# Zero products in TensorE's gaps, queries made token by token, and x in a ring of ten tiles, in a planned attention and GeGLU kernel

## The chip, the cores and the metric

One core of a Trainium2 chip runs the whole kernel. The metric is device time in microseconds of one execution; the time given for a kernel is the median of its runs. TensorE (PE) multiplies, VectorE (DVE), ScalarE (ACT) and GpSimd (POOL) work on elements, SyncE (SP) issues most DMAs.

## What is computed

A transformer block on x of 2048 tokens by 640, in bf16, with 32 query heads of 20 channels that share one key and one value head:

```python
q = (x @ wq).reshape(B, S, H, Dh).transpose(0, 2, 1, 3)     # H = 32, Dh = 20
k, v = x @ wk, x @ wv                                       # one head
p = softmax(einsum("bhqd,bkd->bhqk", q, k) * Dh ** -0.5)
A(x) = einsum("bhqk,bkd->bhqd", p, v).transpose(...) @ wo
B(x) = (gelu(x @ w_gate) * (x @ w_up)) @ w_down             # 640 -> 1536 -> 640
h = x + A(layernorm(x));  out = h + B(layernorm(h))
```

## The kernel before

**A program planned ahead.** The Python code holds a small model of the core. `_Plan` keeps a clock for each engine. A loop (the end of the kernel function) picks the engine that is free first and asks its `*_decide` function for the next piece of work; `commit` books it with an assumed cost, an assumed delay until others see the result, and its dependences. What comes out is a fixed order of instructions for each engine. `resolve` and `emit` turn the dependences into semaphore waits. The assumed costs only shape the order; on the chip each engine runs its list in that order and waits where a semaphore is not there yet. SP's list is in order as well. `PRM` holds the numbers that steer the choice (how many units may be open, how early work may start, ring sizes).

**The work.** The 16 tiles of 128 tokens are normalized (LN1: `ln_group`, `ln_stats`), written to `xn_tmp` and brought into channel-major form in `xn1T` by a DMA transpose. `kv_job` makes keys (`kT4`, four copies at partitions 0, 32, 64, 96) and values (`v_ext`, with a column of ones that yields the softmax's sum, and in three weights). The square root in LN1 is a power on POOL; while any power is outstanding (`pow_left`), `dve_ok` keeps DVE from exponentials, since the power and the 64-bit add are both POOL operations.

**Attention.** It is cut into 64 *units* of 256 query columns for each of four heads, each of 8 *packs* of two key tiles: 512 packs. A pack (`issue_qk`, L912) is eight products of 20 rows by 256 columns, in the four row groups of the array, into four PSUM banks. Each bank is a *tile* of 512 exponentials. Either ACT takes it (`act_tile`, L1266, into the ring `pa` of `NA` = 26 slots), or DVE does (`dve_tile`, L1325, one multiply and add into a 16-bit integer that is read as bf16, into the ring `pd` of `ND` = 9 slots), and POOL then adds two constants to it (L1405) so that three weighted versions cancel the error. The products with values (`issue_pv`, L975) are two per ACT tile and six per DVE tile, of 32 output columns each, so four run side by side in the column groups. A unit's sums lie in one bank, go to `osb`, are transposed by DMA to `onu`, divided (L634), collected in `onq`, transposed to `onT` and multiplied by `wo`.

**Side work.** Pieces of other products (`mm`, L502) fill PE between packs: queries, output projection, and per *batch* of tiles gate, up and down. `mm` splits each product of 128 weight columns in four of 32, one for each column group, which is also how the value products use the array. `SW` is the time the plan books for a change between the two ways. `q_job` makes the queries of a pair of units with the channels on the partitions: weights `wq`, moving operand `xn1T`, 20 of 32 columns used, so that the result can be copied straight into `qT`, of `NQ` = 3 slots. All 16 tiles of x stay in `xh`, to which first `wo`'s result (L676) and then the down product (L798) are added in place. LN2 puts its result in a buffer of its own, `xn2T`.

**The head and the tail.** x and the attention weights are loaded on the queues of SP and ACT at the start, the other weights on SP when the plan's clock for SP has passed 30 us. The tail is what is left once no pack is left: the last batches (tiles 12 and 13; 14; 15). Their gate and up products move 256 and 128 columns.

Of the kernel before, what the change touches and what calls it, by code (L numbers as in the profile page):

```python
# [37 lines left out]
class _Plan:  # L38
# [104 lines left out]
    def emit(self, name, eng, sems):  # L143
        done = 0
        for op, waits in zip(self.ops[name], self.waits[name]):
            for d in waits:
                if d.dma:
                    eng.wait_ge(d.sem, 16)
# [28 lines left out]
class _Job:  # L177
# [14 lines left out]
PRM = {  # L192
    "chunks": [[0], [1], [2, 3], [4, 5], [6, 7], [8, 9], [10, 11], [12, 13], [14], [15]],
# [3 lines left out]
    "NA": 26, "ND": 9, "NON": 4,  # L197
    "open": 3, "open_head": 3, "acc_head": 2, "w_head": 4, "w_max": 2, "w_tol": 600.0,
    "early": 530.0, "slack": 60.0, "open_r": 14, "press_a": 5, "press_d": 2, "v_min": 2,
    "q_ahead": 2, "lay": 0, "flex_d": 400.0, "pair_min": 4, "age": 3000.0, "pool_max": 3000.0,  # L200
    "stag_n": 3, "stag_w": 250.0,
    "quota": 3,
    "rate": 350.0, "w_tol0": 0.0, "w_max0": 2, "lag": 20, "quota0": 4, "quota_n": 16,
# [3 lines left out]
def bass_sequential_preLN__grouped_kv_mqa__glu_gated_geglu__prompt_kernel(  # L207
# [35 lines left out]
    NQ = 3  # L243
# [12 lines left out]
    xh = sb("xh", [P, NT, D], BF16)  # L256
    xn1T = sb("xn1T", [P, NC_D, S], BF16)
    xn2T = sb("xn2T", [P, NC_D, 1024], BF16)
    wq_sb = sb("wq_sb", [P, NC_D * D + 16], BF16)
# [6 lines left out]
    qT = sb("qT", [P, NQ, 512], BF16)  # L266
# [10 lines left out]
    ident = sb("ident", [P, P], BF16)  # L277
# [8 lines left out]
    ln_r = sb("ln_r", [P, 2, NT], F32)  # L286
    nwt = sb("nwt", [P, 4, NT], F32)
    pd16 = pd[:].bitcast(BF16)
# [33 lines left out]
    load("sp", xh[:, 0, :], x_view[:, 0, :], [("x", 0)], lat=2000)  # L322
    load("act", xh[:, 1, :], x_view[:, 1, :], [("x", 1)], lat=2200)
    load("sp", wk_v, cview(A_wk), ["wk"], lat=2500)
    load("act", wv_sb[:], cview(A_wv), ["wv"], lat=2500)
    load("sp", xh[:, 2:4, :], x_view[:, 2:4, :], [("x", 2), ("x", 3)], lat=2800)
    load("act", wq_v[:, :, 0:HALF], cview(A_wq)[:, :, 0:HALF], [("wq", 0)], lat=4000)
    load("sp", xh[:, 4:6, :], x_view[:, 4:6, :], [("x", t) for t in range(4, 6)], lat=4000)
    load("act", wq_v[:, :, HALF:D], cview(A_wq)[:, :, HALF:D], [("wq", 1)], lat=4500)
    load("sp", xh[:, 6:8, :], x_view[:, 6:8, :], [("x", t) for t in range(6, 8)], lat=5000)  # L330
    load("sp", xh[:, 8:12, :], x_view[:, 8:12, :], [("x", t) for t in range(8, 12)], lat=6000)
    load("sp", xh[:, 12:16, :], x_view[:, 12:16, :], [("x", t) for t in range(12, 16)], lat=8000)
# [4 lines left out]
    pool(lambda e: e.memset(warm[:], 0.0), 80, writes=["warm"])  # L337
    pool(lambda e: e.memset(halfc[:], 0.5), 80, writes=["halfc"])
    pool(lambda e: e.memset(wk_sb[:, NC_D * Dh:NC_D * Dh + 16], 0.0), 80, writes=["wkz"])
    pool(lambda e: e.memset(wq_sb[:, NC_D * D:NC_D * D + 16], 0.0), 80, writes=["wqz"])  # L340
# [3 lines left out]
    pool(lambda e: e.memset(ident[:], 0.0), 120, writes=["ident0"])  # L344
    pool(lambda e: e.affine_select(out=ident[:], in_=ident[:], compare_op=ALU.not_equal, fill=1.0, base=0,
                                   pattern=[[-1, P]], channel_multiplier=1), 320, ["ident0"], ["ident"])
# [10 lines left out]
    slots = {"xt": list(range(NXT)), "q": list(range(NQ)), "onT": list(range(4)), "osb": list(range(NOS)),  # L357
             "onu": list(range(NOS))}
# [21 lines left out]

    def ln_stats(ln, t, prio, then):
        key = ("x", t) if ln == 0 else ("h", t)

        def b(op):
            dve(lambda e: e.bn_stats(stats[:, ln, t, 6:12], xh[:, t, HALF:D]), 360, [key], [("st", ln, t, 1)],  # L385
                prio, c)
# [5 lines left out]
        dve(lambda e: e.bn_stats(stats[:, ln, t, 0:6], xh[:, t, 0:HALF]), 360, [key], [("st", ln, t, 0)], prio, b)  # L392

    def ln_group(ln, tiles, prio, done):
# [4 lines left out]
        if ln == 0:  # L399
            state["pow_left"] += 1  # L400

        def after_stats(op):
            cnt[0] += 1
            if cnt[0] == n:
                dve(lambda e: e.tensor_copy(ln_vb[:, ln, sl], mv[:, ln, sl, 1]), 65,
                    [("mv", ln, t) for t in tiles], [("vb", kk)], prio, c2)

        def c2(op):
            dve(lambda e: e.tensor_scalar_add(ln_veb[:, ln, sl], ln_vb[:, ln, sl], EPS), 65,
                [("vb", kk)], [("veb", kk)], prio, c3 if ln == 0 else n0)  # L410

        def c3(op):
            def pdone(op):
                state["pow_left"] -= 1
                c4(op)
            task(("pool",), lambda e: e.tensor_tensor(ln_denb[:, ln, sl], ln_veb[:, ln, sl], halfc[:, 0:n], ALU.pow),
                 700, L_POOL, [("veb", kk), "halfc"], [("den", kk)], prio, pdone)
# [4 lines left out]
        def n0(op):  # L422
            dve(lambda e: e.tensor_copy(va, ln_veb[:, ln, sl]), 65, [("veb", kk)], [("nv", kk)], prio, n1)

        def n1(op):
            dve(lambda e: e.tensor_scalar(ya.bitcast(I32), va.bitcast(I32), -0.5, 1597463007.0, ALU.mult, ALU.add),
                65, [("nv", kk)], [("ny", kk)], prio, newton(0))

        def newton(i):
            def s1(op):  # L430
                dve(lambda e: e.scalar_tensor_tensor(ta, va, -0.5, ya, ALU.mult, ALU.mult), 65,
                    [("nv", kk), ("ny", kk)], [("nt", kk)], prio, s2)

            def s2(op):
                dve(lambda e: e.tensor_tensor(ta, ta, ya, ALU.mult), 65, [("nt", kk), ("ny", kk)], [("nt", kk)],
                    prio, s3)

            def s3(op):
                dve(lambda e: e.scalar_tensor_tensor(ya, ta, 1.5, ya, ALU.add, ALU.mult), 65,
                    [("nt", kk), ("ny", kk)], [("ny", kk)], prio, newton(i + 1) if i < 2 else nden)  # L440
            return s1

        def nden(op):
            dve(lambda e: e.tensor_tensor(ln_denb[:, ln, sl], va, ya, ALU.mult), 65, [("nv", kk), ("ny", kk)],
                [("den", kk)], prio, c4)

        def c4(op):
            dve(lambda e: e.reciprocal(ln_r[:, ln, sl], ln_denb[:, ln, sl]), 75, [("den", kk)], [("lr", kk)],
                prio, c5)

        def c5(op):
            for t in tiles:
                norm(t)

        def norm(t):
            slot = []

            def then(op):
                s = slot[0]

# [4 lines left out]
                if ln == 0:  # L465
                    o = xn1T[:, :, t * P:(t + 1) * P]
                    wkeys = [("xn1T", t)]
                else:
                    o = xn2T[:, :, xcol[t]:xcol[t] + P]
                    wkeys = [("xn2T", xcol[t])]  # L470
# [4 lines left out]
            tk = _Task(("dve",), None, 350, L_DVE, [key, ("lr", kk)], [], prio, then, lambda: bool(slots["xt"]))  # L475

            def bind():
                s = slots["xt"].pop(0)
                slot.append(s)
                tk.fn = lambda e: e.tensor_scalar(xn_tmp[:, s, :], xh[:, t, :], mv[:, ln, t, 0:1],  # L480
                                                  ln_r[:, ln, t:t + 1], ALU.subtract, ALU.mult)
# [8 lines left out]
    xcol = {}  # L490
    for b, tl in enumerate(BATCHES):
        for i, t in enumerate(tl):
            xcol[t] = (b % 2) * 512 + i * P

# [3 lines left out]
    def mm(o, l, r, st, sp):  # L498
        def fn(e, b):
# [3 lines left out]
            return ins  # L503
        return fn

    def col4(a):
        return lambda q: a[:, 32 * q:32 * q + 32]

    def kv_job(tiles):
# [3 lines left out]
        for c in range(NC_D):  # L513
            pieces.append((mm(lambda b: bank(b, n), (lambda c: lambda q: wk_sb[:, c * Dh:c * Dh + 32])(c), xn1T[:, c, t0 * P:t0 * P + n],
                              c == 0, c == NC_D - 1), c_mm(n), [("xn1T", t) for t in tiles] + ["wk", "wkz"]))
# [30 lines left out]
    for ci, tl in enumerate(CHUNKS):  # L546
        nt = len(tl)
        G = 2 // nt
        for k in range(NG // G):
            units.append({"id": len(units), "chunk": ci, "tiles": tl, "groups": list(range(k * G, (k + 1) * G)),  # L550
                          "left": list(range(NT // 2)), "q": None, "qop": None, "acc": None, "npk": 0,
# [3 lines left out]
    def q_job(ua, ub):  # L555
        tl, gs = ua["tiles"], ua["groups"] + ub["groups"]
        n = len(tl) * P
        t0 = tl[0]
        pieces = []
        for gi, g in enumerate(gs):  # L560
            for c in range(NC_D):
                pieces.append((mm((lambda gi: lambda b: ps[:, b * 512 + gi * n:b * 512 + (gi + 1) * n])(gi),
# [964 lines left out]
```

## Time and profile before

| | |
|---|---|
| median of 3 runs | 824.82 us (818.34 to 826.53) |
| the profiled execution | 823.09 us, its span 821.2 us |
| mean granted TensorE clock | 0.954 |
| PE, DVE, ACT, POOL busy | 737.2, 678.4, 699.3, 567.9 us |
| products on PE | 18392, each with a weight load |
| packs (eight products each), tiles of ACT and DVE | 512; 1287 and 761 |

The profile is of one execution. A *span* runs from the first to the last instruction; what the execution takes beyond it lies around the instructions. *Idle before* is the time an engine stood still ahead of an instruction, and the *releaser* is what ended that; "issue" means that the profile shows nothing it waited for. The *chain* follows the work that ended last back from the end. *PEclk* is the TensorE clock that was granted, as a share of full speed. A product's record is longer than the time until the next may start, so the busy time of PE overstates how full the array is.

### The profile page before, as it was taken

To read this page: it belongs to the slowest core of one execution; us is meant where nothing else is said; L and a number is where in the kernel's file an instruction comes from. 1 tells how busy PE (TensorE), PEld (TensorE's weight loads), DVE (VectorE), ACT (ScalarE), POOL (GpSimd) and SP (SyncE) were. 2 spreads that over 40 slices of the span, in tenths; PEclk is the share of its full clock that TensorE was granted. 3 is DMA by queue.
4 is the path that set the end of the run, shared out by engine and by line. 5 is a ranking of instruction groups with operands and counts; after the bars stand their busy time and mean duration, and the time that the engine had idled before them with its cause. 6 is when DMAs were issued, how large, how long until landed. Compare 5 with 4: busy or idle time off the path is not lost.

```text
span 821.2 us, 41718 instructions
## 1 busy us (share of the span) xinstructions
PE 737.2 (90%) x18392; PEld 408.6 (50%) x18392; DVE 678.4 (83%) x1389; ACT 699.3 (85%) x1231; POOL 567.9 (69%) x1424
## 2 busy tenths in 40 slices
PE   2788999988898999999999998999998999999976
PEld 2444444444443455355555444455545554465874
DVE  5756789998888888898899989998899899899532
ACT  1888799988888999999998999999999899999411
POOL 2265788887877786688887785788887784678100
PEclk9776899998988999999999999999999999999999
DMA  8880000001100201100101000100101010111110
GB/s 207 106 320 9 17 10 18 9 9 25 21 13 10 25 10 20 25 10 10 34 10 50 10 10 19 26 9 10 34 10 42 18 26 4 26 18 38 31 29 20
DMA packets 60452, 27.57 MB, mean 34 GB/s; under 512 B 51440, under 2 KB 58992, under 8 KB 60272
## 3 DMA queue, kind: packets, MB, share of 16 engines
q1 hardware_dynamic: 58160, 23.89, 13.6%
q8 instruction: 146, 2.39, 1.2%
q10 hardware_dynamic: 2112, 1.01, 0.5%
q14 instruction: 34, 0.28, 0.1%
HBM read 10.21 MB, written 2.62 MB: 16 GB/s over the span
## 4 chain that ended last, share of the span: by engine, by line
PE 47%; DVE 31%; ACT 13%; issue 4%; DMA 3%; POOL 2%; SPq 0%; POOLq 0%
DVE pd L1325 22%; PE ps L502 18%; PE ps L975 16%; PE ps L912 12%; ACT pa L1266 10%; POOL pd L1405 1%; ACT gbuf L764 1%; DMA onu<-osb 1%; DVE onq L634 1%; DMA xn2T<-xn_tmp 1%; DVE qT L378 1%; DVE gbuf L779 1%; DMA onT<-onq 1%; DVE osb L1011 1%; DVE stats L385 1%
## 5 line engine op out<-in xcount | busy, mean ns | idle before, releaser
L1266 ACT ACTIVATE pa<-ps 128x512 bf16<-128x512 f32 (+1 forms) x1120 | 649.3, 694 | 55.9 <-PE ps L912 43.6
L1405 POOL INT64_ADD pd<-pd x1402 | 560.5, 419 | 170.9 <-DVE pd L1325 153.2
L1325 DVE TENSOR_SCALAR pd<-ps 128x512 uint16<-128x512 f32 x761 | 484.9, 681 | 72.7 <-PE ps L912 63.7
L975 PE MATMUL ps<-pd,v_ext 128*32 128x256 bf16 x4566 | 276.6, 286 | 9.1 <-DVE pd L1325 4.1
L912 PE MATMUL ps<-qT,kT 20*128 20x256 bf16 x4096 | 248.3, 281 | 34.0 <-DVE pd L1325 18.1
L975 PE MATMUL ps<-pa,v_ext 128*32 128x256 bf16 x2574 | 234.1, 288 | 4.1 <-ACT pa L1266 1.4
L975 PEld LDWEIGHTS ps<-pd,v_ext 128*32 128x32 bf16 x4566 | 163.5, 99 | 66.3 <-issue 31.4
L912 PEld LDWEIGHTS ps<-qT,kT 20*128 20x128 bf16 x4096 | 81.0, 93 | 195.5 <-DVE pd L1325 103.3
L975 PEld LDWEIGHTS ps<-pa,v_ext 128*32 128x32 bf16 x2574 | 126.1, 100 | 37.8 <-issue 19.6
L502 PE MATMUL ps<-xn2T,wu_sb 128*32 128x512 bf16 (+2 forms) x1440 | 70.6, 312 | 5.4 <-issue 5.2
L502 PE MATMUL ps<-xn2T,wg_sb 128*32 128x512 bf16 (+2 forms) x1440 | 70.1, 309 | 5.3 <-issue 4.6
L502 PE MATMUL ps<-wd_sb,gbuf 128*32 128x320 bf16 x1536 | 68.3, 301 | 0.5 <-issue 0.4
L502 PE MATMUL ps<-xn1T,wq_sb 128*32 128x256 bf16 (+1 forms) x1600 | 52.3, 261 | 18.0 <-DMA xn1T<-xn_tmp 15.7
L779 DVE TENSOR_TENSOR gbuf<-ps,gbuf 128x512 bf16<-128x512 f32 (+2 forms) x72 | 36.4, 508 | 25.7 <-PE ps L502 16.1
L502 PEld LDWEIGHTS ps<-xn1T,wq_sb 128*32 128x32 bf16 x1600 | 33.9, 100 | 31.6 <-DMA xn1T<-xn_tmp 15.7
L502 PEld LDWEIGHTS ps<-wd_sb,gbuf 128*32 128x32 bf16 x1536 | 39.2, 96 | 16.6 <-issue 9.6
L748 ACT ACTIVATE gbuf<-ps 128x128 bf16<-128x128 f32 (+1 forms) x36 | 11.3, 313 | 37.6 <-PE ps L502 37.6
L502 PEld LDWEIGHTS ps<-xn2T,wg_sb 128*32 128x32 bf16 x1440 | 31.5, 96 | 21.9 <-issue 12.8
L502 PEld LDWEIGHTS ps<-xn2T,wu_sb 128*32 128x32 bf16 x1440 | 31.3, 97 | 22.4 <-issue 13.2
L502 PE MATMUL ps<-wo_sb,onT 128*32 128x320 bf16 x640 | 29.5, 310 | 1.6 <-DMA onT<-onq 1.3
L798 DVE TENSOR_TENSOR xh<-xh,ps 128x320 bf16<-128x320 bf16 x32 | 15.4, 480 | 11.9 <-PE ps L502 11.9
L634 DVE TENSOR_TENSOR onq<-onu,rcp 128x160 bf16<-128x160 bf16 (+1 forms) x56 | 24.4, 454 | 0.3
(50 smaller groups left out, 259.9 us busy)
## 6 DMA issues: line engine op xcount, KB each, us to landing
out_dram<-xh SPq DMA_DIRECT2D x16, 160.0 KB, 1.8
wg_sb<-in_B_w_gate_dram SPq DMA_DIRECT2D x1, 1920.0 KB, 10.9
wu_sb<-in_B_w_up_dram SPq DMA_DIRECT2D x1, 1920.0 KB, 15.3
wd_sb<-in_B_w_down_dram SPq DMA_DIRECT2D x1, 1920.0 KB, 19.9
xh<-in_A_x_dram SPq DMA_DIRECT2D x2, 640.0 KB, 9.9
xh<-in_A_x_dram SPq DMA_DIRECT2D x3, 320.0 KB, 6.3
wq_sb<-in_A_wq_dram ACTq DMA_DIRECT2D x2, 400.0 KB, 9.3
wo_sb<-in_A_wo_dram SPq DMA_DIRECT2D x1, 800.0 KB, 5.4
```

The source lines that it names most:

```text
L378: return e.tensor_copy(o, i)
L385: dve(lambda e: e.bn_stats(stats[:, ln, t, 6:12], xh[:, t, HALF:D]), 360, [key], [("st", ln, t, 1)], prio, c)
L502: ins = e.matmul(o(b)[32 * q:32 * q + 32], l(q), r, start=st, stop=sp, tile_position=(0, 32 * q))
L634: dve((lambda o, vi, ri: lambda e: e.tensor_tensor(o, vi, ri.unsqueeze(3).to_broadcast([P, vi.shape[1], 4, Dh]), ALU.mult))(o, vi, ri), c_ ...
L748: task(("act",), lambda e: e.activation(o, bank(bk, n), ACT.Gelu_apprx_tanh), ("gelu", c_act(n)), L_ACT, [("b", bk)], gkeys(b, fc), 1.0, fin2)
L779: dve(lambda e: e.tensor_tensor(o, bank(bk, n), o, ALU.mult), c_dve(n), [("b", bk)] + gkeys(b, fc), gkeys(b, fc), 0.8, fin)
L798: dve(lambda e: e.tensor_tensor(xh[:, t, h * HALF:(h + 1) * HALF], xh[:, t, h * HALF:(h + 1) * HALF], bank(bk, HALF), ALU.add), c_dve(HALF ...
L912: ins = e.matmul(ps[:, b * 512 + h * 256:b * 512 + h * 256 + 256], kT4[32 * r:32 * r + Dh, kt * P:(kt + 1) * P], qT[32 * r:32 * r + Dh, s, ...
L975: ins = e.matmul(ps[32 * r:32 * r + 32, ab * 512:ab * 512 + 256], v_ext[:, it["kt"], it["w"], :], it["ap"], start=st, stop=(j in ends), ti ...
L1266: op = plan.commit("act", lambda e: e.activation(dst, src, ACT.Exp, scale=SM_SCALE), cost, L_ACT, [("b", b0 + i) for i in range(n)], [("pa ...
L1325: op = plan.commit("dve", lambda e: e.tensor_scalar(pd[:, 0, s * 512:(s + 1) * 512], bank(b), CH_A, CH_B, ALU.mult, ALU.add), c_dve(512), ...
L1405: op = plan.commit("pool", (lambda w, a, sh: lambda e: e.int64_add(pd64[:, w, a], pd64[:, 0, a], sh))(w, a, sh), k * 128 * 1.7 + 180.0, L_ ...
```

## The change

- **Zero products.** `pe_decide` gets a last resort: where nothing else fits, packs are left, a bank is free, and PE was used less than 60% of the last 3.4 us by the plan (`pe_use`), it issues four products of a buffer of zeros into that bank. Nothing reads them.
- **Queries token by token.** `q_job(t, h)` makes half of the channels of one tile with the tokens on the partitions: weights are `xn1T`'s columns, `wq` moves, 320 columns, five products. The result is copied to `qtok` with heads padded from 20 to 32, and a DMA transpose on SP brings it to `qT`, now four slots of one tile. A unit needs `q_ready` of its tiles and halves; a pack's moving operand is a view of one or two slots.
- **x in a ring.** `xh` has ten slots. Tiles 10 to 15 are loaded once tiles 0 to 5 have been normalized. For the residual sum tiles 0 to 5 and 10 to 15 are loaded a second time, when LN1 and the keys are done and, from tile 10 on, the tile ten before has been written out. `xn2T` is gone: LN2's result goes to `xn1T`.
- **The head.** wq, wk and wv are loaded on SP's queue, between the tiles of x; only tile 1 stays on ACT's. LN1's groups from tile 8 on are of four tiles and find the root by Newton steps on DVE; a dummy 64-bit add on POOL follows the last power. ACT may take LN1's norm in place of DVE. The mask for an identity that nothing used is dropped. Small LN operations go ahead of others on DVE.
- **Full-width products.** `mm` issues one product of 128 weight columns in place of four of 32 where no pack is left, and before pack 24, except for keys.
- **Planner.** `NA` 24, `ND` 13; other numbers of `PRM`; ACT and DVE keep their last two ring slots for the oldest unit; a second accumulator may open when slots run short. DMA semaphores are shared by transfers that follow one another.

```diff
 PRM = {
-    "NA": 26, "ND": 9, "NON": 4,
-    "open": 3, ... "w_max": 2, "w_tol": 600.0, "early": 530.0, ... "press_a": 5, "press_d": 2, "v_min": 2,
-    ... "age": 3000.0, "stag_w": 250.0,
+    "NA": 24, "ND": 13, "open": 2, "w_max": 3, "w_tol": 1300.0, "early": 400.0, "press_a": 3, "press_d": 3,
+    "v_min": 3, "age": 1500.0, "res_a": 2, "res_d": 2, "pow_t": 8, "m_head": 24, "z_tail": 0, "z_use": 0.6,
+    "ln1g": [[0], [1], [2, 3], [4, 5], [6, 7], [8, 9, 10, 11], [12, 13, 14, 15]], "stag_w": 400.0, ...
...
-    NQ = 3
+    NQ = 4
...
-    def mm(o, l, r, st, sp):
-        def fn(e, b):
+    def mm(o, l, r, st, sp, whole=True):
+        def fn(e, b, m):
+            if m == "m" and whole:
+                return e.matmul(o(b), l(None), r, start=st, stop=sp)
             ins = None
             for q in range(4):
                 ins = e.matmul(o(b)[32 * q:32 * q + 32], l(q), r, start=st, stop=sp, tile_position=(0, 32 * q))
...
-    def q_job(ua, ub):
...
+    def q_job(t, h):
         pieces = []
+        for c in range(NC_D):
+            pieces.append((mm(lambda b: bank(b, HALF), col4(xn1T[:, c, t * P:(t + 1) * P]),
+                              wq_sb[:, c * D + h * HALF:c * D + h * HALF + HALF], c == 0, c == NC_D - 1),
+                           c_mm(HALF), [("xn1T", t), ("wq", h)]))
...
+                sp_tasks.append(_Task(("sp",), lambda e: e.dma_start_transpose(
+                    o, qtok[:, s, :, :].rearrange("p r e -> p (r e)")), 1200, 1500, [("qtok", s)],
+                    [("q", t % NQ, h)], 0.05 if t < 4 else 0.5, tdone))
...
             def pdone(op):
                 state["pow_left"] -= 1
+                if state["pow_left"] == 0:
+                    plan.commit("pool", lambda e: e.int64_add(lib[:, 1, :]..., lib[:, 0, :]..., 0),
+                                6500.0, L_POOL, ["lib0"], ["lib1"])
...
+    for t in range(NXH, NT, 2):
+        sp_tasks.append(_Task(("sp",), ... e.dma_start(xh[:, t - NXH:t - NXH + 2, :], x_view[:, t:t + 2, :]) ...,
+                              lambda: t - NXH in x_norm and t + 1 - NXH in x_norm))
+    for t in list(range(6)) + list(range(NXH, NT)):
+        sp_tasks.append(_Task(("sp",), ... e.dma_start(xh[:, t % NXH, :], x_view[:, t, :]) ...,
+                              lambda: len(x_norm) == NT and state["kv_left"] == 0 and
+                               (t < NXH or t - NXH in x_out)))
...
+        if (state["qk_left"] > 0 or PRM["z_tail"]) and fits(110.0 + swv - slack) and pe_use(t) < PRM["z_use"]:
+            fb = [b for b in free_now if plan.ready("pe", ["zero"], [("b", b)]) <= t]
+            if fb:
+                b = fb[-1]
+                def zfn(e):
+                    for q in range(4):
+                        ins = e.matmul(ps[32 * q:32 * q + 32, b * 512:b * 512 + 256], zero[:, 0:32], zero[:],
+                                       start=True, stop=True, tile_position=(0, 32 * q))
+                    return ins
+                plan.commit("pe", zfn, 110.0 + swv, L_PE, ["zero"], [("b", b)], at=t)
+                return True
         return False
+
+    def pe_use(t):
+        u = 0.0
+        for op in reversed(plan.ops["pe"]):
+            if op.end < t - 3400.0:
+                break
+            u += op.end - max(op.t0, t - 3400.0)
+        return u / 3400.0
...
-        sw = 0.0 if state["mode"] == "v" else SW
-        state["mode"] = "v"
+        md = "m" if fn.whole and (state["qk_left"] == 0 or state["npack"] < PRM["m_head"]) else "v"
+        sw = 0.0 if state["mode"] == md else SW
+        state["mode"] = md
```

More of the change, by code (lines that the diff above doesn't have):

```diff
@@ L196 @@
     "ln2g": [[0, 1], [2, 3], [4, 5], [6, 7], [8, 9], [10, 11], [12, 13], [14], [15]],
-    "NA": 26, "ND": 9, "NON": 4,
[L198 to L201, printed above, removed]
-    "quota": 3,
-    "rate": 350.0, "w_tol0": 0.0, "w_max0": 2, "lag": 20, "quota0": 4, "quota_n": 16,
+    "NA": 24,
+    "ND": 13,
+    "NON": 4,
+    "open": 2,
+    "open_head": 3,
+    "acc_head": 2,
+    "w_head": 4,
+    "w_max": 3,
+    "w_tol": 1300.0,
+    "early": 400.0,
+    "slack": 60.0,
+    "open_r": 14,
+    "press_a": 3,
+    "press_d": 3,
+    "v_min": 3,
+    "q_ahead": 2,
+    "lay": 0,
+    "flex_d": 400.0,
+    "pair_min": 4,
+    "age": 1500.0,
+    "pool_max": 3000.0,
+    "res_a": 2,
+    "res_d": 2,
+    "ln1g": [[0], [1], [2, 3], [4, 5], [6, 7], [8, 9, 10, 11], [12, 13, 14, 15]],
+    "pow_t": 8,
+    "m_head": 24,
+    "z_tail": 0,
+    "z_use": 0.6,
+    "stag_n": 3,
+    "stag_w": 400.0,
+    "quota": 3,
+    "rate": 350.0,
+    "w_tol0": 0.0,
+    "w_max0": 2,
+    "lag": 20,
+    "quota0": 4,
+    "quota_n": 16,
 }
@@ L329, in bass_sequential_preLN__grouped_kv_mqa__glu_gated_geglu__prompt_kernel, with xk @@
[L329 to L332, printed above, removed]
+    def xk(*ts):
+        return [("x", t) for t in ts] + [("xs", t % NXH) for t in ts]
+    load("sp", xh[:, 0, :], x_view[:, 0, :], xk(0), lat=2900)
@@ L343, in bass_sequential_preLN__grouped_kv_mqa__glu_gated_geglu__prompt_kernel @@
              writes=[("vone", w)])
[L344 to L346 removed]
+    for i in range(2):
+        plan.commit("dve", (lambda i: lambda e: e.memset(qtok[:, i, :, :].bitcast(F32), 0.0))(i), 300, L_DVE, (),
+                    [("qtok", i)])
     plan.commit("act", lambda e: e.activation(warm[:, 0:1], warm[:, 1:2], ACT.Exp), 1500, L_ACT,
@@ L570, in fin @@
             def fin(op):
-                ua["qop"] = op
-                ub["qop"] = op
                 free_bank(b)
-            flex_copy(qT[:, s, :], bank(b), 512, [("b", b)], [("q", s)], 0.6, fin)
-        def gate():
-            if not slots["q"]:
-                return False
-            for v in units[:ua["id"]]:
-                if v["q"] is None:
-                    return False
-            return True
-        jobs.append(_Job(("q", ua["id"]), 1.0, pieces, then, gate))
+                s = qs[0]
@@ L941, in issue_qk @@
             u["closed"] = True
-            if hq == 1:
-                slots["q"].append(s)
+            for x in u["tiles"]:
+                if q_last[x] == u["id"]:
+                    q_owner[x % NQ] = None
         state["npack"] += 1
@@ L1090, in pe_decide @@
         opening = None
-        if nxt_u is not None and may and (len(accu) < (PRM["acc_head"] if head else 1)):
+        if nxt_u is not None and may and (len(accu) < (PRM["acc_head"] if head or press else 1)):
             q2 = pv_lists(t, [nxt_u])
@@ L1099, in pe_decide @@
         piece = next_piece(t, may, pick_bank)
+        if piece is None and not may and free_now and len(wb) < 4 and len(active) < 2:
+            piece = next_piece(t, True, pick_bank)
+            if piece is not None and piece[2] >= 0.85:
+                piece = None
         wready = nr >= 1 or opening is not None or piece is not None
@@ L1301, in act_decide @@
                 return True
+        if rd and pa_free.count(True) <= PRM["res_a"]:
+            u0 = min(u["id"] for u in open_units())
+            rd = [x for x in rd if x["u"]["id"] == u0]
         if not rd:
@@ L1475, in _ @@
             plan.emit("sp", e, sems)
[L1476 to L1477 removed]
+            for op in outs:
+                e.wait_ge(op.sem, op.count)
         @block.scalar
```

258 lines of the change are left out of this document (165 added, 93 removed).

## The prediction

> **What bounds the kernel now.** I read the page's head first, then the busy time by stage, cut by me where the stages change: first scores at 19.6 us, end of the half-speed stretch at 83.3, first MLP work at about 329, last scores at 763.9.
>
> ```profile
> span 821.2 us, 41718 instructions
> ...
> PE 47%; DVE 31%; ACT 13%; issue 4%; DMA 3%; POOL 2%; SPq 0%; POOLq 0%
> ```
>
> ```profile
> 0.00:19.60 19.60, 3.92 (x208) 3.89 (x208) 10.95 (x46) 2.92 (x11) 4.05 (x18) 1.00 0.76 212
> 19.60:83.30 63.70, 51.30 (x1272) 28.03 (x1260) 40.05 (x102) 51.19 (x94) 31.21 (x75) 0.73 0.60 141
> 83.30:329.00 245.70, 222.97 (x4856) 113.70 (x4848) 215.86 (x417) 220.48 (x376) 196.62 (x471) 0.92 0.09 16
> 329.00:763.90 434.90, 414.94 (x10220) 223.08 (x10212) 390.46 (x757) 412.08 (x716) 335.92 (x862) 1.00 0.10 21
> 763.90:821.20 57.30, 44.13 (x1870) 39.93 (x1864) 21.04 (x68) 12.61 (x38) 0.06 (x1) 0.99 0.11 27
> ```
>
> The columns are the stretch, its length, busy us of PE, PEld, DVE, ACT and POOL with their counts, then the granted clock. Nothing is idle for long between 83 and 764: ACT is busy 94.8% of the last long stage, DVE 89.8%, PE 95.4%. The exponentials on ACT and DVE set the pace there, and PE follows closely, since its chain share is the largest. Three places are worse than this. From 19.6 to 83.3 DVE works 40.05 of 63.7 us. Before 329 the clock is 0.73 and 0.92. After 763.9 only PE matters, yet it idles 13 us.
>
> The granted clock explains two of these.
>
> ```profile
> 158.40:161.80 3.40, 2.23 (x36) 0.60 (x24) 3.40 (x7) 3.40 (x8) 3.01 (x8) 1.00 0.00 0
> 161.80:165.20 3.40, 3.19 (x56) 1.83 (x60) 2.96 (x8) 2.47 (x4) 3.14 (x6) 0.50 0.03 5
> ```
>
> After a stretch of 3.4 us with 36 products, in which PE had work for two thirds of the time, the next 3.4 us run at half clock, and ACT falls from 3.40 to 2.47 us of work. I summed all half-clock stretches from 76.5 to 329 (first row) and the full-clock stretches between them (second), and the same from 32.1 to 76.5 (third and fourth).
>
> ```profile
> sum 47.70, PE 46.55 PEld 22.51 DVE 30.68 ACT 32.02 POOL 33.67; mean PE 4.65 PEld 2.25 DVE 3.07 ACT 3.20 POOL 3.37
> sum 204.80, PE 183.22 PEld 94.50 DVE 188.86 ACT 192.98 POOL 168.34; mean PE 20.36 PEld 10.50 DVE 20.98 ACT 21.44 POOL 18.70
> sum 27.30, PE 24.13 PEld 13.15 DVE 11.79 ACT 22.74 POOL 10.66; mean PE 8.04 PEld 4.38 DVE 3.93 ACT 7.58 POOL 3.55
> sum 17.10, PE 13.25 PEld 6.57 DVE 14.11 ACT 15.06 POOL 12.35; mean PE 4.42 PEld 2.19 DVE 4.70 ACT 5.02 POOL 4.12
> ```
>
> At full clock ACT and DVE are busy (192.98 + 188.86) / 2 / 204.8 = 93.2%; at half clock 65.7%, with PE full. There PE is the bound. The chain of the tail shows the third place.
>
> ```profile
> 789.86 1.45 issue
> 791.30 1.97 PE ps L502 x128
> 793.27 1.78 issue
> ...
> 797.02 1.38 issue
> ...
> 804.32 1.30 issue
> ...
> 807.65 1.44 issue
> ...
> 811.06 1.77 issue
> ```
>
> PE waits for nothing the profile shows, and between two such gaps lie 128 products, with their loads 256 instructions. The gaps come where products stream only 128 columns. I read them as PE running out of fetched instructions. The six shown are 9.1 us.
>
> **The change, part by part.**
>
> *Full-width products in the tail.* One product with 128 weight columns replaces four with 32, so a quarter of the instructions is fetched per time and the gaps should go: -9.1 us. Against it stand the weight loads. A group of four narrow products of 128 columns takes 1.97 / 32 = 0.062 us. A full-width one has its own load of 128 columns. The only such loads in the trace are those of the scores:
>
> ```profile
> L912 PEld LDWEIGHTS ps<-qT,kT 20*128 20x128 bf16 x4096 | 81.0, 93 | 195.5 <-DVE pd L1325 103.3 <-issue 44.2 <-ACT pa L1266 18.4
> ```
>
> If loads hide entirely the product still takes 62 ns; if each paces its product, 93. Tiles 14 and 15 have 2 x 24 x 5 = 240 such products, so the price is 0 to 240 x 31 ns = 7.5 us. I take the middle, 3.8, since loads overlap products but here are back to back. Tail: -5.3, bounds -9.1 and -1.6. Products of 256 and 320 columns outlast a load.
>
> [...]
>
> *Zero products.* Where the plan sees PE used under 60% in its last 3.4 us and a bank is free, four zero products are put in. If every half-clock stretch ran at the utilization of its full-clock neighbours, the first would take (32.02 + 30.68) / 2 / 0.932 = 33.6 us instead of 47.7, saving 14.1; those of the head (22.74 + 11.79) / 2 / 0.853 = 20.2 instead of 27.3, saving 7.1. The bounds are 0 and -21.2. The zero products are placed by planned times and the chip drifts from these, so I take two thirds: -14. Their own cost:
>
> ```profile
> 310.49 0.33 PE ps L912 x8
> 310.82 1.10 PE ps L975 x36
> ```
>
> Four products of 256 columns take 1.10 / 9 = 0.12 us, and eight for scores 0.33 instead of 0.24, so some 0.1 more at a change of kind. That lies in gaps where PE waits for ACT and DVE. If PE is late against its plan there, each costs up to 0.22 us, and it also waits for the last reader of its bank, with all later products queued behind.
>
> [...]
>
> *The head.* DVE may take exponentials only when no power is outstanding on GpSimd. Powers are now needed for tiles 0 to 7 alone, and a dummy 64-bit add afterwards starts what now delays the first real one.
>
> ```profile
> 11.16 0.28 POOL L345 TENSOR_SCALAR_AFFINE_SELECT ident<-ident 128x128 bf16<-128x128 bf16 x1 [9.50 <-issue]
> ...
> 19.47 0.69 POOL L416 TENSOR_TENSOR ln_denb<-ln_veb,halfc 128x2 bf16<-128x2 bf16 x1 [2.00 <-DVE ln_veb L409]
> ...
> 31.91 0.69 POOL L416 TENSOR_TENSOR ln_denb<-ln_veb,halfc 128x2 bf16<-128x2 bf16 x1 [1.75 <-DVE ln_veb L409]
> 38.55 9.09 POOL L1405 INT64_ADD pd<-pd  x22 [5.94 <-DVE pd L1325]
> ```
>
> The fifth power, of tiles 6 and 7, ends at 20.2 instead of the last at 32.6, so DVE is free for exponentials 12 us earlier. With a delay of 5.9 to 9.5 us GpSimd is ready at 26 to 30 instead of 38.6; the adds queued behind it are covered by 13 slots. [...] DVE was not idle from 20 to 32, it normalized; ACT may now take norms. The stage's work at 93.2% would fit in (51.19 + 40.05) / 2 / 0.932 = 48.9 us of 63.7, a gain of 14.8, of which 7.1 was counted for the clock: bounds 0 and -7.7, taken -4.
>
> *Queries token by token.* Before, 8 jobs of 20 groups at 0.062 and 24 jobs of 10 at 0.12 make 39 us of PE; now 32 jobs of 5 groups of 320 columns, 0.15 by the same rate, make 24. PE saves 15, worth at most its chain share, 7. Copies shrink from 512 to 320 columns:
>
> ```profile
> L1011 DVE CAST osb<-ps 128x256 bf16<-128x256 f32 x48 | 19.9, 415 | 3.1 <-PE ps L975 3.1
> ...
> L378 DVE CAST qT<-ps 128x512 bf16<-128x512 f32 x27 | 18.4, 681 | 0.6 <-PE ps L502 0.6
> ```
>
> ```profile
> 12.98 2.65 DMA xn1T<-xn_tmp
> ```
>
> ```profile
> 12.98 25.34 SPq L471 DMA_TRANSPOSE xn1T<-xn_tmp  x16
> ```
>
> 320 lie at about 481 ns, so 32 x 0.2 = 6.4 us of two engines, 3.2 of time. Together -3 to -10, taken -5. New is a DMA transpose per half tile, 2.65 us behind the copy, on SP, where one follows another every 25.34 / 16 = 1.58 us. Four tile slots cover it: a pair's 64 packs run while the next pair is prepared. Only the first is bare: a shorter product phase but a copy and 2.65 us more, so the first scores come 0 to 3 us later, taken +1.
>
> *Rings and parameters.* DVE waits 5.1 us for its ring of nine:
>
> ```profile
> DVE pd L1325 <- PE ps L975: 5.1, 7, 2.4
> ```
>
> Thirteen end most of that, and two fewer ACT slots give some back: -2, bounds -5 and +3. The x ring adds 3 loads of two tiles and 12 of one. They wait on SP, each for a norm or for an output written hundreds of us earlier, with transposes queued behind; nothing, unless several come late; then each delays the transposes behind it. The planner's other numbers reorder everything. No row prices that; the two long stages at 93.2% would take 664.6 us instead of 680.6, so 16 us is the most to gain, clock included, and I allow as much the other way and take 0.
>
> **Sum.** -5.3 - 14 - 4 - 5 + 1 - 2 = -29.3. From the profiled execution's 823.1 (span 821.2 and 1.9 around it) that gives 793.8. This execution lies 1.7 under the median of 824.8, so I forecast 795, with 778 to 810 as its own range.
>
> **The rivals.** *The clock still falls*: zeros are put where the plan idles and not where the chip does, or do not count as activity. For it: the profile has no such product. Against: short gaps fill exactly the stretches shown. Without the -14: 809.
>
> *Weight loads pace the tail*: full-width products run at 93 ns or more. For it: they are the only loads without narrow neighbours. Then the tail gains 1.6: 799. [...]
>
> *Queries come late*, the slower case: SP is in order, so a query transpose behind one that waits for a late output block stops the scores at a tile's start. Each of the 32 half tiles then costs 2.65 us. Eleven late ones eat the gain; with sixteen, 795 + 42 = 837. Against: the four slots.
>
> **Chances.** Forecast 0.52, clock 0.20, loads 0.14, late queries 0.14. About 1% is what a measurement of this kernel can tell from no change. The forecast and the loads lie beyond it, the clock case mostly (809 is 1.9% down), late queries on the other side: faster 0.75, same 0.12, slower 0.13. The range leaves out the late queries and the far ends: 768 to 828.
>
> **What would show it.** Right: a granted clock near 1.0 from 35 us on, no gaps behind 128 products in the tail, tail under 53 us, DVE exponentials before 30 us, scores by 21 us, no score product waiting on the query transposes. Wrong: half-clock stretches beside zero products, tail products 93 ns apart, score products waiting for DMA, or ACT under 90% between 83 and 764 at full clock, which would lay the time on the new order.

## The result, and the profile after

The changed kernel takes 795.75 us (median of 4 runs, 794.10 to 798.73), the kernel before 821.71 in the same session (4 runs): a ratio of 0.968, interval 0.962 to 0.975. The forecast of 795 is met. It will turn out that its terms are not: three of them failed and two others made up for that. A run more than 1.5% above the fastest of its kernel in its session counts as slow and is left out of the ratios and of the table below (four of the kernel before, two of the kernel before with a wide tail).

The head of the changed kernel's page, from the profiled execution (798.73 us): its span, the granted clock in 40 slices, the chain by engine.

```profile
span 796.9 us, 37265 instructions
...
PEclk8688899978899899999999998999999999999999
...
PE 52%; DVE 28%; ACT 11%; DMA 6%; issue 2%; SPq 1%; POOL 0%; DVEq 0%
```

The clock still falls in the first third of the span; "issue" has halved. By stage, in the columns explained with the prediction (the cuts are the first scores at 21.7, pack 32 of 512 at 88.1, the same 329, and the last scores just before 751.4):

```profile
0.00:21.70 21.70, 16.66 (x329) 11.34 (x329) 14.14 (x57) 5.84 (x14) 4.35 (x17) 0.84 0.75 194
21.70:88.10 66.40, 53.09 (x936) 26.07 (x934) 42.72 (x128) 47.93 (x83) 29.55 (x65) 0.74 0.67 166
88.10:329.00 240.90, 226.87 (x4984) 116.88 (x4984) 220.81 (x422) 221.99 (x382) 207.12 (x480) 0.94 0.14 23
329.00:751.40 422.40, 410.75 (x9470) 215.29 (x9458) 379.27 (x760) 400.90 (x706) 329.66 (x835) 0.99 0.14 27
751.40:796.90 45.50, 42.62 (x477) 36.44 (x476) 21.59 (x69) 12.21 (x37) 0.00 (x0) 1.00 0.11 30
```

The tail is 45.5 us instead of 57.3, with PE idle for 2.9 us instead of 13.2. The half-clock stage is no shorter (66.4 against 63.7) and its clock no higher (0.74 against 0.73). When each pack's first score product starts tells the rest:

| us at pack | 0 | 32 | 64 | 128 | 256 | 384 | 511 | span |
|---|---|---|---|---|---|---|---|---|
| before | 19.7 | 80.4 | 126.1 | 213.1 | 396.4 | 577.9 | 762.0 | 821.2 |
| after | 21.8 | 88.1 | 126.3 | 212.6 | 387.9 | 571.9 | 748.5 | 796.9 |

The head loses 7.7 us by pack 32 and has them back at 64; packs 128 to 511 gain 13, the tail 11.

### The profile page after: what moved, and what is told of

Same layout as the page of the kernel before. It is cut to its first block, busy times and chain, and to the rows that moved or that the text cites. A ratio compares the mean times of both kernels' runs of the same rounds, so it can differ in the third digit from the quotient of the medians.

```text
span 796.9 us, 37265 instructions
## 1 busy us (share of the span) xinstructions
PE 750.0 (94%) x16170; PEld 406.0 (51%) x16170; DVE 678.5 (85%) x1432; ACT 688.9 (86%) x1217; POOL 570.7 (72%) x1396
## 4 chain that ended last, share of the span: by engine, by line
PE 52%; DVE 28%; ACT 11%; DMA 6%; issue 2%; SPq 1%; POOL 0%; DVEq 0%
DVE pd L1462 20%; PE ps L1073 18%; PE ps L1009 15%; PE ps L563 12%; ACT pa L1400 10%; PE ps L560 6%; DMA onu<-osb 2%; DMA onT<-onq 1%; DVE onq L715 1%; PE ps L1280 1%; DMA xn1T<-xn_tmp 1%; DVE stats L434 1%; DMA qT<-qtok 1%; DVE osb L1109 1%; DVE xh L757 1%
## 5 line engine op out<-in xcount | busy, mean ns | idle before, releaser
L1400 ACT ACTIVATE pa<-ps 128x512 bf16<-128x512 f32 (+1 forms) x1104 | 634.0, 715 | 51.6 <-PE ps L1009 43.8
L1009 PE MATMUL ps<-qT,kT 20*128 20x256 bf16 x4096 | 263.8, 281 | 29.5 <-DVE pd L1462 13.1
L563 PE MATMUL ps<-wd_sb,gbuf 128*32 128x320 bf16 x1104 | 53.0, 302 | 0.3 <-DVE pd L1462 0.2
L563 PE MATMUL ps<-xn1T,wg_sb 128*32 128x512 bf16 x720 | 50.2, 382 | 0.1
L563 PE MATMUL ps<-xn1T,wu_sb 128*32 128x512 bf16 x720 | 49.0, 381 | 0.2
L563 PEld LDWEIGHTS ps<-wd_sb,gbuf 128*32 128x32 bf16 x1104 | 23.4, 95 | 18.8 <-issue 12.2
L1280 PE MATMUL ps<-zero 128*32 128x256 bf16 x460 | 23.0, 334 | 4.1 <-POOL halfc L376 1.0
L563 PEld LDWEIGHTS ps<-xn1T,wu_sb 128*32 128x32 bf16 x720 | 16.4, 96 | 18.0 <-issue 6.3
L882 DVE TENSOR_TENSOR xh<-xh,ps 128x320 bf16<-128x320 bf16 x32 | 15.3, 479 | 11.1 <-PE ps L560 11.1
L1109 DVE CAST osb<-ps 128x256 bf16<-128x256 f32 x47 | 19.5, 414 | 6.0 <-PE ps L1073 5.9
L563 PEld LDWEIGHTS ps<-xn1T,wg_sb 128*32 128x32 bf16 x720 | 15.4, 95 | 16.9 <-issue 7.8
## 6 DMA issues: line engine op xcount, KB each, us to landing
wu_sb<-in_B_w_up_dram SPq DMA_DIRECT2D x1, 1920.0 KB, 11.1
```

Source lines behind the costliest of these rows:

```text
L563: ins = e.matmul(o(b)[32 * q:32 * q + 32], l(q), r, start=st, stop=sp, tile_position=(0, 32 * q))
L882: dve(lambda e: e.tensor_tensor(xh[:, t % NXH, h * HALF:(h + 1) * HALF], xh[:, t % NXH, h * HALF:(h + 1) * HALF], bank(bk, HALF), ALU.add) ...
L1009: ins = e.matmul(ps[:, b * 512 + h * 256:b * 512 + h * 256 + 256], kT4[32 * r:32 * r + Dh, kt * P:(kt + 1) * P], qv[32 * r:32 * r + Dh], s ...
L1109: return e.tensor_copy(o, i)
L1280: ins = e.matmul(ps[32 * q:32 * q + 32, b * 512:b * 512 + 256], zero[:, 0:32], zero[:], start=True, stop=True, tile_position=(0, 32 * q))
L1400: op = plan.commit("act", lambda e: e.activation(dst, src, ACT.Exp, scale=SM_SCALE), cost, L_ACT, [("b", b0 + i) for i in range(n)], [("pa ...
```

## The granted clock between runs of one kernel

This must be known to read the experiments. In the profiles of the kernel before and of the changed one a stretch is granted either full or half clock (14 and 12 stretches at 0.50, all others at 1.00). Taken so for every run, its half-clock time is 2 x (1 - mean clock) x span: 75.6 us for the profiled kernel before (clock 0.954). It differs from run to run of the same program. Over all 47 runs of the kernel before that the experiments brought along, the mean clock went from 0.936 to 0.969, and the 15 runs with the lowest clock averaged 94.9 us at half clock and 827.0 us of time, the 15 with the highest 65.9 and 819.1. The straight line through all 47 is 0.28 us of time for a us of half clock (interval 0.24 to 0.32, correlation 0.91); through the 43 that the table counts it is 0.26. That is the price the prediction worked out: 14.1 of 47.7 us is 0.30, 7.1 of 27.3 is 0.26. It is a correlation: no experiment sets the clock by itself.

So beside each measured time stands what it would be at 75 us of half clock, from the runs' means by that line.

| kernel | median us, runs | ratio to before, interval | mean us | half-clock us | at 75 |
|---|---|---|---|---|---|
| before | 822.0, 43 | 1 | 822.4 | 77.9 | 821.6 |
| after, once more | 796.8, 6 | 0.966, 0.962 to 0.970 | 796.2 | 68.3 | 798.1 |
| after, tail products narrow | 810.9, 6 | 0.984, 0.980 to 0.989 | 810.4 | 79.8 | 809.1 |
| after, no zero products | 794.5, 6 | 0.965, 0.961 to 0.969 | 795.1 | 77.0 | 794.5 |
| after, no zero products at the start | 796.0, 6 | 0.965, 0.960 to 0.969 | 794.9 | 61.1 | 798.8 |
| after, query products doubled | 815.8, 10 | 0.995, 0.993 to 0.998 | 816.2 | 80.3 | 814.7 |
| after, MLP weights later | 793.1, 6 | 0.964, 0.960 to 0.968 | 792.4 | 70.6 | 793.6 |
| after, old planner numbers | 807.6, 6 | 0.981, 0.976 to 0.985 | 807.3 | 72.8 | 807.9 |
| before, wide tail | 802.4, 4 | 0.977, 0.973 to 0.981 | 802.9 | 60.1 | 807.1 |
| before, new planner numbers | 812.6, 10 | 0.987, 0.983 to 0.991 | 812.2 | 56.0 | 817.6 |
| before, wide tail and new numbers | 803.1, 6 | 0.975, 0.971 to 0.980 | 802.8 | 61.2 | 806.7 |
| before, two fifths of the query products left out | 823.7, 12 | 1.001, 0.998 to 1.005 | 823.3 | 97.1 | 817.1 |
| after, weights later, no zeros at the start | 788.5, 6 | 0.958, 0.954 to 0.962 | 788.6 | 55.6 | 794.1 |

## Experiments on the tail

*Narrow products in the tail of the changed kernel*, same plan:

```
+        me = "v" if state["qk_left"] == 0 else md
-        plan.commit("pe", lambda e: fn(e, b, md), ...)
+        plan.commit("pe", lambda e: fn(e, b, me), ...)
```

> The changed kernel with the same order; only after the last pack each full-width product is issued as four of 32 columns again. If the gaps behind each 128 products were what the tail lost, they come back: the tail grows from 45.5 to 54 to 58 us and the time by 9 to 12 us. If the full-width products were worth nothing in themselves and the tail shrank through its new order, the time moves by less than 3 us.

Measured: 14.1 us above the changed kernel in the same session, more than the 9 to 12 expected. The chain of its tail, in order of time (start, length, what):

```profile
771.27 2.04 PE ps L563 x128
773.31 1.44 issue
774.75 1.97 PE ps L563 x128
776.72 1.77 issue
778.49 1.97 PE ps L563 x128
780.46 1.66 issue
782.12 5.73 PE ps L563 x256
787.85 1.21 issue
789.07 1.97 PE ps L563 x128
791.03 1.77 issue
792.81 1.97 PE ps L563 x128
794.78 1.77 issue
```

The gaps behind 128 products are back. In the changed kernel the same part of the chain is two lines without one:

```profile
751.48 38.84 PE ps L560 x447
790.67 3.45 PE ps L560 x24
```

*Wide products in the tail of the kernel before*, same plan:

```
+            if wide:
+                return e.matmul(o(b), l(None), r, start=st, stop=sp)
...
+        wide = state["qk_left"] == 0
```

> The kernel before with its own plan, instruction for instruction, except that once the last score product is placed each product group goes as one instruction of 128 weight columns in place of four of 32. If the fetch of instructions is what the tail pays for, the gaps behind every 128 products go and the tail shortens by 9 to 14 us: 808 to 813 against 823. If a weight load of 128 columns paces the products at 93 ns, it shortens by under 3 us: 820 or more.

Measured: 19 us below before (0.977 of 821.5 in that session), more than the 10 to 15 expected, while the tail by itself keeps within its 9 to 14. Its tail, from the last score product to the end, is 803.7 - 757.4 = 46.3 us in the trace, against 821.2 - 762.1 = 59.1: 12.8 less. The other 6 lie ahead of the tail, where both kernels issue the same instructions; at equal clock the gain is 14.5 (821.6 to 807.1), so clock accounts for most of them.

Three pairs of traces that differ in the width alone thus give 13.8 (62.0 against 48.2, in the changed kernel), 12.8, and 13.3 (60.7 against 47.4, with the new numbers in both).

Two things put the gaps down to the fetching of instructions. With a quarter of the instructions for the same products the gaps, 9.6 us in the six shown, are gone. And the profile has the transfers themselves: a DMA queue of kind "instruction", here in the changed kernel with narrow products in the tail and then in the changed kernel (packets, MB, share):

```profile
q8 instruction: 140, 2.29, 1.2%
```

```profile
q8 instruction: 128, 2.10, 1.1%
```

Each packet holds 16 KB, and there is about one for 256 instructions of PE: 17604 products with their loads make 137.5 times 256, and 16170 make 126.3. In the narrow tail every one of the six gaps begins 0.8 to 1.1 us after such a packet starts (at 772.40, 775.88, 779.63, 786.75, 790.12 and 793.86 us) and ends 1.2 to 1.5 us after it is through. The packet at 783.26, among down products of 320 columns (96 in 3.48 us), leaves none. The gap's period, 128 products with their loads, is as many instructions as one packet stands for.

What a wide product takes is read from the timeline of the changed kernel's tail (start, length, what):

```profile
774.87 0.72 PE L560 MATMUL ps<-xn1T,wu_sb 128*128 128x128 bf16 x10
775.43 0.72 PE L560 MATMUL ps<-xn1T,wg_sb 128*128 128x128 bf16 x10
775.99 0.72 PE L560 MATMUL ps<-xn1T,wu_sb 128*128 128x128 bf16 x10
```

Ten start every 0.56 us, so one takes 56 ns, less than a narrow group's 62. Ten with 256 moving columns take 1.09 us, and 48 with 320 take 6.52 (136 ns each), so the time goes by the moving columns, and no cost of the loads of 128 columns shows. A load's record isn't its pace: on the page of before the loads of 32 columns last 95 to 100 ns, no less than the 93 of those of 128, though a narrow product follows every 15 ns. The 93 ns that paced the prediction's bound doesn't show in the rate.

## Experiments on the zero products and the clock

*No zero products*, same plan, their instructions not issued (the waits ahead of them stay):

```
-                        ins = e.matmul(... zero[:, 0:32], zero[:], ...)
-                    return ins
+                    return None
```

> The changed kernel with the same order of work on every engine; only the 115 groups of zero products are not issued (the waits ahead of them stay). Theory 1 (the zero products hold the clock up where they stand): half-clock time grows from 82 us to 95 us or more, and the time by 4 to 10 us. Theory 2 (they run ahead of the gaps they were planned for, and the clock falls anyway): half-clock time stays within 10 us of 82 and the time within 2 us of the changed kernel.

*No zero products ahead of the first real product*: 57 of the 115 groups left out.

```
+                early = not state.get("real")
...
+                    if early:
+                        return None
```

> The changed kernel with the same order; only the zero products ahead of the first real product (57 groups from 1.0 to 10.4 us) are not issued. Theory A (these start the watch on the clock too early: PE is active to 9.5 us, then idle to 13.9, and the clock falls at 12.3): without them the clock stays full until about 30 us as in the kernel before, the first scores come up to 1 us earlier and the time falls by 1 to 4 us. Theory B (the start is bound by the queries' transposes on SP): the first scores move by less than 0.3 us and the time by less than 1 us.

Measured: 794.5 and 796.0, against 796.8 with all of them. The zero products are worth nothing measurable. Why those at the start don't help is seen in the timeline of PE in the changed kernel:

```profile
1.01 8.47 PE L1280 MATMUL ps<-zero 128*32 128x256 bf16 x223 [1.01 <-POOL halfc L376]
9.98 0.38 PE L1280 MATMUL ps<-zero 128*32 128x256 bf16 x5 [0.50 <-issue]
13.89 1.51 PE L560 MATMUL ps<-wq_sb,xn1T 128*128 128x320 bf16 x5 [3.53 <-DMA xn1T<-xn_tmp]
```

The plan spreads them over the head, but on the chip, with nothing to wait for, 223 run at once in 8.47 us, PE then idles 3.5 us, and the clock on record is at half (0.50 from 13.8 to 15.5 us) when the queries begin. Without them it is full there, in the version that is run last (first row; the second is the changed kernel's):

```profile
13.70:20.00 6.30, 6.22 (x70) 3.50 (x71) 5.46 (x22) 2.10 (x9) 0.70 (x1) 1.00 0.93 202
```

```profile
13.80:20.00 6.20, 6.11 (x70) 3.41 (x71) 5.37 (x22) 2.10 (x9) 0.70 (x1) 0.57 0.98 208
```

At clock 1.00 and at 0.57 the same 70 products take the same 6.1 to 6.2 us, so little was lost by it. With only the zeros at the start left out the first scores come 1 us earlier in the trace (20.8 against 21.8), but the time doesn't fall. The zero products further on do act on the clock: with them alone the half-clock time is 61.1 us, without any 77.0. At 0.28 this is 4.5 us. The times are equal all the same, so their own cost seems to take about as much (a difference of two means; that cost wasn't measured by itself). The traces fit this: with all zero products pack 64 comes at 126.3 and 127.0 us and 670.6 and 665.4 us follow, without any at 129.7 and 662.6 follow.

## Experiments on the queries

*Query products doubled* in the changed kernel, same plan:

```
+        if jb.name[0] == "q":
...
+                    ins = e.matmul(bank(b, HALF)[32 * q:32 * q + 32], zero[:, 0:32], wq_sb[:, 0:HALF],
+                                   start=False, stop=False, tile_position=(0, 32 * q))
```

> The changed kernel, same plan, with each narrow query product group followed by four products of 320 columns with zero weights into the same bank: some 24 us more of TensorE, none of it in other engines. If the lighter queries are where the middle of the kernel gains (TensorE's share of the chain at about one half), this costs 9 to 13 us: 805 to 810. If exponentials pace the middle and TensorE has the slack, under 4 us: below 801.

*Two fifths of the query products left out* in the kernel before, same plan:

```
-        fn = pc[0]
+        fn = (lambda e, b: None) if jb.name[0] == "q" and jb.pos % NC_D in (1, 2) else pc[0]
```

> The kernel before with its own plan, except that of each query group's five products along the contraction two are left out (640 of 1600 instructions; the queries are sums over three fifths of the model dimension). TensorE does some 16 to 20 us less, as in the change, and nothing else moves. If the lighter queries gain what the doubled ones cost (21 us for 25 us of TensorE), the time falls by 11 to 17 us: 805 to 811. If exponentials pace the kernel before, it falls by under 4 us: 818 or more. My prediction's price was 3 to 10 us: 812 to 819.

The two don't say the same. 24 us more cost about 20, more than either expectation had: first scores come at 31.8 us, 10 later, and by pack 511 another 8 to 13 have come on top (766.5 against 748.5 and, in the second trace, 744.0). Some 15 us less are worth nothing: 823.7 against 822.6 for the kernel before beside it. Two windows of that second run show what changed:

```profile
104.00:129.00 25.00, 22.81 (x442) 10.60 (x434) 20.44 (x37) 21.87 (x39) 20.25 (x46) 0.86 0.04 8
129.00:213.00 84.00, 73.09 (x1520) 36.02 (x1518) 75.47 (x148) 71.92 (x128) 70.94 (x162) 0.88 0.09 15
```

```profile
104.00:129.00 25.00, 22.96 (x491) 11.55 (x492) 21.07 (x37) 22.80 (x40) 20.28 (x49) 0.93 0.04 8
129.00:213.00 84.00, 73.91 (x1600) 38.10 (x1598) 76.70 (x150) 74.01 (x130) 72.16 (x165) 0.90 0.08 15
```

The second pair is the kernel before. With fewer products (442 and 1520 against 491 and 1600) the clock is lower, and ACT and DVE get no more done. Over 12 runs the half-clock time is 97.1 us, against 77.3 in the 16 runs of before in that session. By the line this is 5.5 us, and at equal clock the lighter queries give 4.5 (821.6 to 817.1). So work taken off PE was paid back in clock, as far as the line prices it. What this run leaves out is products alone; the smaller copies of the new queries, 3.2 us of the prediction's term, were not tested.

## Experiments on the order and the head

*The planner numbers alone*, in the kernel before (nine, though the expectations say eight: open, w_max, w_tol, early, press_a, press_d, v_min, age and stag_w as in the diff):

> The kernel before with the eight planner numbers of the changed one (open 2, w_max 3, w_tol 1300, early 400, press 3 and 3, v_min 3, age 1500, stagger 400); its own queries, rings, head and tail. The order of all work changes. If these numbers make the middle's gain, packs 64 to 511 take 7 to 14 us less and the time is 809 to 816; if the gain is from lighter queries or longer rings, it is 819 to 827, or slower where an order made for another kernel fits worse.

*The same with the wide tail*:

> The kernel before with two parts of the change together: the eight planner numbers and full-width products in the tail. No zero products, no queries token by token, rings of 9 and 26, the old head. If the parts add up (10 and 18 us measured apart), this is 792 to 797, the same as the changed kernel, and its other parts come to nothing together. If the tail is worth 13 and the order is chance, it lies at 800 to 810.

*The changed kernel with the old numbers* (and res_a, res_d at -1):

> The changed kernel with the old planner numbers (the eight, and no reserve of ring slots). If the new numbers are worth 10 us here as they are in the kernel before, 803 to 808. If they are worth nothing beside the other parts, 793 to 798.

Measured: 812.6, 803.1 and 807.6. The first gains 10 us, and most of it is clock (4 are left at 75 us of half clock). Its windows over the stretch where the kernel before had 0.93 and 0.90:

```profile
104.00:129.00 25.00, 24.06 (x566) 13.03 (x560) 24.12 (x43) 24.79 (x48) 22.84 (x50) 1.00 0.10 20
129.00:213.00 84.00, 77.89 (x1780) 41.06 (x1778) 80.97 (x158) 81.91 (x155) 74.54 (x168) 1.00 0.12 17
```

ACT is busy for 81.91 of 84 us instead of 74.01, and pack 128 starts at 196.1 instead of 213.1. The order kept the clock up here where zero products were meant to. The clock stays up in the trace with the new numbers and the wide tail, too (none at half from 83.3 to 233 us, pack 128 at 199.3). Later it loses again: packs 256 to 511 take 370.8 us instead of 365.6.

With the wide tail in all four, the numbers and everything else in the change stand in a square (ratio to before):

| | old head, queries, rings, no zeros | as changed |
|---|---|---|
| old numbers | 0.977 | 0.981 |
| new numbers | 0.975 | 0.966 |

Each interval is 0.004 to 0.005 to either side. Neither half is worth anything measurable alone; together they take 9 us (0.977 to 0.966; 807.1 to 798.1 at equal clock). Where they do is seen in the traces, one or two for each cell. Pack 64 comes at 122.5 and 120.9 us with the old head and at 129.8 and 126.3 (127.0) as changed. From there to the end it is 681.2 and 681.4 us in the left column, 675.3 with the old numbers and everything else, and 670.6 (665.4) with both. So what everything else gains later with the old numbers, the head loses first. That 10 and 18 would add up wasn't borne out. Why the two need each other isn't settled, and neither is which number does it: changing any of them makes another order of the whole plan, and one order each was run.

*MLP weights later*: wg, wu and wd issued after the plan's 80 us instead of 30.

```
-                              [], [nm], 9.0, None, lambda: plan.free["sp"] > 30000.0))
+                              [], [nm], 9.0, None, (lambda lim: lambda: plan.free["sp"] > lim)(
+                                  30000.0 if nm == "wo" else 80000.0)))
```

> The changed kernel with the loads of wg, wu and wd issued after the plan's 80 us instead of 30 us; all else in the plan's order. If the first output transposes are late because these three loads are ahead of them in the DMA engines, the idle 6.2 to 6.6 us of DVE, ACT and PE near 69 to 75 us goes, pack 32 comes 4 to 7 us earlier (81 to 84), and the time falls by 3 to 6 us below the changed kernel. If the stall has another source, or what is late there is made up by the exponentials afterwards anyway, the time stays within 2 us of it.

Measured: 793.1. The waits of the changed kernel from 66 to 80 us (who waited for whom; us, times, longest), and the DMA issues from 50 to 75 (KB, median us to landing):

```profile
ACT pa L1400 <- PE ps L1009: 8.0, 3, 6.2
POOL pd L1545 <- DVE pd L1462: 7.9, 3, 6.5
PEld ps L1009 <- DVE pd L1462: 7.3, 3, 6.5
DVE rcp L720 <- DMA onu<-osb: 6.6, 1, 6.6
```

```profile
wd_sb<-in_B_w_down_dram SPq DMA_DIRECT2D x1, 1920.0 KB, 16.0
xh<-in_A_x_dram SPq DMA_DIRECT2D x3, 160.0 KB, 5.4
qT<-qtok SPq DMA_TRANSPOSE x1, 6.3
onu<-osb SPq DMA_TRANSPOSE x1, 10.6
```

DVE's reciprocal waits 6.6 us (67.2 to 73.8, with nothing else run on DVE) for the first output transpose, which is issued at 63.2 us and takes 10.6 while the loads of wu and wd are under way (they land 11.1 and 16.0 us after their issue). PE, ACT and POOL then wait up to 6.5 us for DVE or behind it. The loads of wu and wd have the same condition in the code as before, but go out at 55.3 and 55.8 us instead of 39.6 and 40.1: on SP the query transposes (the last at 52.5) and the second loads of x (at 47.0 and 53.7) now come ahead of them. With the weights later no output transpose takes more than 4.7 us, the longest wait of that reciprocal is at most 1.7 us, and pack 32 comes at 81.2 instead of 88.1. At pack 64 it is 125.6 against 126.3 in the changed kernel, and of the 7 us 3.7 are left in the median, within what the intervals allow to be nothing. The cause of the stall is shown; its cost, about half its length in the medians, is not settled.

*Weights later and no zero products at the start*, both edits as above:

> The changed kernel with the loads of wg, wu and wd after 80 us and without the zero products ahead of the first real product. If the two gains seen apart (3 us in the time from the loads, 1 to 2 us in the first scores without the zeros) add up, 789 to 792 and first scores near 21; if both are within what runs differ by, 793 to 797.

788.5 us, ratio 0.958 (0.954 to 0.962), the fastest of all: 4.2% below the kernel before and some 7 us below the changed one (0.966, 0.962 to 0.970; the two were not run side by side, and the intervals just touch). From 22 to 88 us it has a clock of 0.92 where the changed kernel (second row) has 0.74, and ACT and DVE get 24 us more done between them:

```profile
22.00:88.00 66.00, 58.56 (x1239) 31.27 (x1231) 54.56 (x148) 59.53 (x104) 42.27 (x94) 0.92 0.51 89
```

```profile
22.00:88.00 66.00, 52.70 (x927) 25.89 (x919) 42.32 (x126) 47.80 (x82) 29.55 (x65) 0.74 0.67 165
```

By its half-clock time of 55.6 us and the line, 3.6 us of the gain over the changed kernel are clock. The rest, some 4, is about what the later weights brought by themselves.

## Why the prediction was right, point by point

- *Full-width products, -5.3: too small.* 12.8 to 13.8 measured. The step that failed is the +3.8 for weight loads, taken halfway between 62 and 93 ns: 56 was measured. The 93 is the length of a load's record, which narrow loads have as well (95 to 100 ns), and no pace. The gaps were under-counted too: I took the six on the chain, 9.1 us, when the stage's row already had 13 us of idle PE, of which 10.3 went.
- *Zero products, -14: failed.* The price of half-clock time was right (0.26 to 0.30 assumed, 0.28 seen). The amount was not: "the chip drifts from these, so I take two thirds" was far too much, for a product that waits for nothing but its bank isn't held to its planned time (223 ran in 8.47 us). The changed kernel's 10 runs have 69.9 us at half clock against 77.9 before, 2.2 us by the line. And their own cost, put at nothing, seems to take back what the later ones gain. The first rival's mechanism came true in the main, its 809 did not.
- *Queries, -5: failed for the products, open for the copies.* I multiplied 15 us of PE by PE's share of the chain. That share says what the time passed through, not what less of it would bring: lighter queries alone brought nothing, and the clock fell with them. What the smaller copies brought, and whether the queries are what the new numbers need, is open.
- *Head, -4 and +1: failed in sum.* DVE's exponentials start at 27.0 us (32.5 before) and GpSimd's first add at 27.8 (38.6), as the steps said. The first scores are 2.1 us later in the two profiles, within the 0 to 3 allowed (19.7 to 22.2 us in the five traces with the old head, 20.8 to 22.8 in the eight with the new one and queries not doubled). But the weights held up the first output transpose, and pack 32 comes 7.7 us later; that I had not priced: the loads have the same condition in the code, and I did not ask what SP now issues ahead of them and what lands beside them.
- *Rings, -2: not tested.* DVE's 5.1 us of waiting for its ring are gone from the trace; what that is worth by itself no run shows.
- *Planner numbers, 0 within 16: the largest miss beside the clock.* Old numbers cost the changed kernel 11 us; by themselves they are worth 1 to 10.
- *Weight loads pace the tail*: false, by the 56 ns. *Queries come late*: the chain has query transposes for 1% of the span, one of them 4.13 us at 477.8; nothing like 16 of them.

In short: -14 and -4 did not come and -5 isn't shown to have come, the tail gave some 8 more, and the order and its interplay with the rest 9 to 11 that were put at nothing. The sum was met by chance. What held was the range, which the unknown order had made wide.

## What to carry to other kernels

Where a stage has gaps of "issue" at a fixed count of instructions (256 here), look for packets of the instruction queue at their start, use fewer and larger instructions (12.8 to 13.8 us here), and count all idle time of that engine in the stage, not the pieces that the chain shows (13.2 us against 9.1). Before a saving on TensorE is priced, look at the granted clock: with two fifths of the query products left out, half-clock time was 97.1 us instead of 77.3, so compare kernels by clock as well as by time. A filler instruction must wait on something that happens at the moment it is meant for (223 of these ran in the first 9.5 us); and a load that nobody needs yet should not stand ahead of a transfer on which an engine waits (6.6 us of DVE here).

## What was not expected of the hardware

- The mean granted clock of one program varied from 0.936 to 0.969 between runs, and carried most of the spread of its time (4.0 us standard deviation, 1.7 once the line is taken off).
- In the tail PE stopped for 1.2 to 1.8 us behind each 128 narrow products of 128 columns, each time 0.8 to 1.1 us after a 16 KB packet of the instruction queue had started.
- The first query products run at the same pace at a granted clock of 1.00 as at 0.50, five of 320 columns in 1.5 us (0.3 each); in the tail one product of 320 columns takes 0.136. So the 1.00 on record there isn't borne out by the pace.
- An output transpose that costs the chain 4.31 us where no load is under way (at 552.17 us) took 10.6 from 63.2 us on, with two loads of 1.9 MB landing at 66.4 and 71.8.
